# Linear attention and a routed feed-forward in one kernel: sixteen weight loads and three stores moved along one hand-written transfer queue, two tiles issued from a second one

## The chip, the cores and the metric

One Trainium2 chip, one of its cores. A time is the device time of one execution in microseconds (us), the median of the runs shown. TensorE is written PE, VectorE DVE, ScalarE ACT, GpSimd POOL; SP is the SyncE engine, which computes nothing here and only issues transfers.

## The reference, cut to what matters

q, k and v are (4, 8, 768, 64) in fp32: 4 batches, 8 heads, 768 positions, head size 64. Then a router takes the 128 best rows of each batch through a feed-forward with 1024 hidden units.

```python
for b in range(nb):                                   # blocks of 64 positions
    intra = einsum('bhic,bhjc->bhij', qb, kb) * Dmask # decayed causal scores
    intra = einsum('bhij,bhjd->bhid', intra, vb)
    inter = einsum('bhid,bhde->bhie', qb * lam_pow, kv_state)
    out[:, :, sl] = intra + inter
    kv_state = lam_block * kv_state + einsum('bhsd,bhse->bhde', kb * rev_pow, vb)
x = out.transpose(0, 2, 1, 3).reshape(B, S, 512)
scores = x @ w_gate
for b in range(B):
    top = argpartition(-scores[b], 128)[:128]
    ye = maximum(x[b, top] @ w1, 0) @ w2              # w1 512x1024, w2 1024x512
    out[b, top] = x[b, top] + sigmoid(scores[b, top])[:, None] * ye
```

## The kernel before, in words

**Groups.** The work is cut into 24 groups g of 128 positions, six for each batch. A group needs three tiles, kn, qn and vn (k, q and v of its positions, all heads), each 256 KB, read in pieces of 256 bytes. `load(g)` (L71) issues the three, in this order. The pool `ld` has six buffers of each, so `load(g)` has to wait until group g - 6 is done with its own.

**The main loop (L673).** Iteration g finishes group g and prepares group g + 1. Groups 0 to 8 run in a "wide" form (128 positions at a time), later ones in a narrow form (two halves of 64). On PE an iteration of the wide form goes: transposes of q and k of group g + 1 (L204); the state product of group g + 1 (L271, or L280 for the first narrow group; needs vn of g + 1, and k decayed by POOL, `kd`, L188); scores times v of group g (L335); scores of g + 1 (L231); the share of the state (L323); the row of gate scores (L405, once in each iteration).

**The feed-forward.** When a batch's six groups are done, its 128 rows are found, and POOL fetches them from the output in DRAM by an indirect transfer (`xs`, L480), so all six stores of that batch must have landed. `expert` then hands out pieces that stand between the narrow iterations: transposes of `xs` (L493), eight hidden chunks f = 0 to 7 (L530; chunks 0 to 3 need the first four weight transfers, chunks 4 to 7 the next four), eight output chunks (L542; each needs one of the last eight). The first batch's pieces begin in iteration 9.

**The transfers.** All loads, weights and stores of whole groups go through one queue, SP's, in the order in which the program issues them. The weights come as 16 transfers of 256 KB (rows of 2 KB), here called w0 to w15 (w1 in w0 to w7, w2 in w8 to w15). Where they stand is written out by hand: `WEIGHTS_WITH` (L50) names the groups behind whose kn or qn load the next weight is issued, and `STORES_WITH` (L51) the loads behind which the store of a finished group (L377, 256 KB) is issued. Stores not named there are issued when the group is finished. ACT's queue carries two small tensors at the start, `lam` and `w_gate` (L86, L88).

**The start.** Iteration -1 prepares group 0. PE transposes k, then q of group 0; ACT copies each out of PSUM (L208); DVE builds the decay masks; POOL makes an identity and a zero tile (L110 to L115), then decays k of groups 0 and 1.

Of the kernel before, what the change touches and what calls it, by code (L numbers as in the profile page):

```python
# [8 lines left out]
FP32 = mybir.dt.float32  # L9
# [8 lines left out]
def kernel(  # L18
# [12 lines left out]
    nc = tc.nc  # L31
# [5 lines left out]
    L = 128  # L37
# [8 lines left out]
    assert 0 <= CAP < S  # L46

    AHEAD = 6
    WIDE = 9
    WEIGHTS_WITH = {"kn": (12, 13, 14), "qn": range(4, 17), "vn": ()}  # L50
    STORES_WITH = {  # L51
        "kn": {5: (0,), 6: (1,), 7: (2,), 8: (3,), 9: (4, 5)}, "qn": {},
        "vn": {11: (6,), 12: (7,), 13: (8,), 14: (9, 10), 15: (11,), 20: (12, 13), 21: (14, 15)},
    }
    PIECES = {13: (1, 0, 1), 14: (1, 0, 1), 15: (1, 0, 2), 20: (1, 0, 1), 21: (1, 0, 1),
# [4 lines left out]
    const = ctx.enter_context(tc.tile_pool(name="const", bufs=1))  # L60
    ld = ctx.enter_context(tc.tile_pool(name="ld", bufs=AHEAD))
    att = ctx.enter_context(tc.tile_pool(name="att", bufs=3))
# [8 lines left out]
    def load(g):  # L71
        b, c = divmod(g, NT)
        rows = slice(c * L, (c + 1) * L)
        tiles = []
        for name, src in (("kn", k), ("qn", q), ("vn", v)):
            t = ld.tile([128, H, D], FP32, name=name)
            nc.sync.dma_start(out=t[:], in_=src[b, :, rows, :].rearrange("h p d -> p h d"))
            tiles.append(t)
            if g in WEIGHTS_WITH[name]:
                weights.pop(0)()  # L80
            for s in STORES_WITH[name].get(g, ()):
                store(s)
        loaded[g] = tiles
# [2 lines left out]
    nc.scalar.dma_start(out=lam_b[:], in_=lam.unsqueeze(0).broadcast_to([128, H]))  # L86
    wg_row = const.tile([1, HD], FP32, name="wg_row")
    nc.scalar.dma_start(out=wg_row[:], in_=moe_w_gate.unsqueeze(0))  # L88
    for g in range(3):
        load(g)  # L90
    wg_b = const.tile([128, HD], FP32, name="wg_b")
# [15 lines left out]
    weights = [w1_load(f0, n, c) for f0 in (0, n) for c in range(NDC)]  # L107
    weights += [w2_load(f) for f in range(NFC)]

    ident = const.tile([128, 128], FP32, name="ident")  # L110
    make_identity(nc, ident)
    zero = const.tile([128, L], FP32, name="zero")
    nc.gpsimd.memset(zero[:], 0.0)
    one_row = const.tile([1, 128], FP32, name="one_row")
    nc.gpsimd.memset(one_row[:], 1.0)  # L115

    su = psum.tile([128, 2, 512], FP32, name="su")
    o_ = psum.tile([128, 2, 512], FP32, name="o")
# [18 lines left out]
    for hp in range(NHP):  # L137
        for hh in range(2):
            h = 2 * hp + hh
            nc.vector.tensor_tensor_scan(  # L140
                out=mask_w[:, hh, hp, :], data0=lam_b[:, h : h + 1].broadcast_to([128, L]),
# [38 lines left out]
    def wide(g):  # L180
        return g < WIDE

# [192 lines left out]
    def store(g):  # L375
        b, t = divmod(g, NT)
        nc.sync.dma_start(  # L377
            out=out[b, t * L : (t + 1) * L, :],
            in_=x_bs[b][:, t].rearrange("p a b e -> p (a b e)"),
        )  # L380
# [261 lines left out]
    def products(n):  # L642
        for _ in range(min(n, len(pieces))):
            pieces.pop(0)()

    def ahead(g):
        return min(4 + max(0, (g - 12) // 2), AHEAD)

# [4 lines left out]
    def loads_to(n):  # L653
        while next_load[0] < min(n, NG):
            load(next_load[0])
            next_load[0] += 1
# [16 lines left out]
    for g in range(-1, NG):  # L673
        loads_to(g + ahead(g))
        if g < 0:
# [9 lines left out]
                out=decay_w[:], in_=qpow[:, :, L - 1 : L].broadcast_to([128, NHP, D])  # L685
# [57 lines left out]
        now = PIECES.get(g, (1, 1, 1))  # L743
        if g == WIDE:
            products(1)
# [101 lines left out]
```

## Time and profile before

| what | value |
|---|---|
| median of 3 runs | 176.89 us (176.65 to 179.35) |
| the profiled execution's own time | 177.37 us |
| its span, first to last instruction | 175.6 us |
| busy share of the span: PE, DVE, POOL, ACT | 91%, 56%, 52%, 41% |
| moved by transfers | 31.96 MB, 182 GB/s over the span |
| mean granted TensorE clock | 0.989 |

All rows come from one profiled execution. A time in a row is counted from the span's start. The profiled execution took 0.48 us more than the median; 1.8 us of its time lies outside the span. Busy shares are averages over stages that have different limits, so the stage of the change has to be looked at by itself.

### The profile page before, as it was taken

To read this page: it belongs to the slowest core of one execution; us is meant where nothing else is said; L and a number is where in the kernel's file an instruction comes from. 1 tells how busy PE (TensorE), PEld (TensorE's weight loads), DVE (VectorE), ACT (ScalarE), POOL (GpSimd) and SP (SyncE) were. 2 spreads that over 40 slices of the span, in tenths; PEclk is the share of its full clock that TensorE was granted. 3 is DMA by queue.
4 is the path that set the end of the run, shared out by engine and by line. 5 is a ranking of instruction groups with operands and counts; after the bars stand their busy time and mean duration, and the time that the engine had idled before them with its cause. 6 is when DMAs were issued, how large, how long until landed. Compare 5 with 4: busy or idle time off the path is not lost.

```text
span 175.6 us, 7861 instructions
## 1 busy us (share of the span) xinstructions
PE 160.3 (91%) x3440; PEld 132.5 (75%) x3440; DVE 98.4 (56%) x227; ACT 71.9 (41%) x192; POOL 91.4 (52%) x101
## 2 busy tenths in 40 slices
PE   6798999873998999999999899999999999989990
PEld 6568888763887899966667799966668888459970
DVE  2577866772595475458546754757567956340011
ACT  2244465541244465454444446544546445003100
POOL 2259974445287842654975953466776800220022
PEclk9999999997899999999999999999999999999999
DMA  4999999998999999999999979999503111021000
GB/s 93 217 219 181 238 228 248 260 231 211 267 234 256 214 295 283 270 276 260 239 240 218 244 168 260 289 241 229 171 14 113 66 63 60 0 60 63 0 30 30
DMA packets 81475, 31.96 MB, mean 182 GB/s; under 512 B 75809, under 2 KB 75809, under 8 KB 81442
## 3 DMA queue, kind: packets, MB, share of 16 engines
q1 hardware_dynamic: 80640, 29.37, 71.2%
q0 software_dynamic: 656, 2.10, 3.7%
q8 instruction: 27, 0.44, 1.1%
q14 instruction: 6, 0.05, 0.1%
q10 hardware_dynamic: 146, 0.01, 0.0%
HBM read 24.12 MB, written 7.34 MB: 179 GB/s over the span
## 4 chain that ended last, share of the span: by engine, by line
PE 75%; DMA 11%; DVE 4%; issue 3%; ACT 2%; SPq 2%; POOLq 1%
PE m L530 18%; PE m L542 13%; PE m L204 10%; PE o L323 6%; PE o L343 5%; PE su L238 4%; PE su L280 4%; PE o L335 4%; DMA vn<-in_v_dram 4%; DMA xs<-out_dram,tok 4%; DMA qn<-in_q_dram 3%; PE m L271 2%; PE m L567 2%; PE su L231 2%; DVE xg L385 2%
## 5 line engine op out<-in xcount | busy, mean ns | idle before, releaser
L530 PE MATMUL m<-xsT,w_sb 128*128 128x128 f32 x256 | 33.8, 281 | 0.5 <-ACT xsT L500 0.5
L415 DVE SCALAR_TENSOR_TENSOR table<-sc_row,sc,lead 128x128 bf16<-128x128 f32 (+5 forms) x24 | 24.8, 1033 | 15.4 <-ACT sc_row L408 14.8
L530 PEld LDWEIGHTS m<-xsT,w_sb 128*128 128x128 f32 x256 | 30.5, 192 | 1.2 <-ACT xsT L500 0.7
L218 POOL TENSOR_TENSOR qs<-qT,qpow 128x512 f32<-128x512 f32 x15 | 20.9, 1391 | 15.0 <-ACT qT L208 14.9
L385 DVE CUSTOM_DVE_ANT_0 xg<-x_b,wg_b 128x512 f32<-128x512 f32 x24 | 22.3, 930 | 9.1 <-ACT x_b L365 8.5
L542 PE MATMUL m<-w_sb,hs 128*128 128x512 f32 x48 | 25.0, 623 | 0.0
L293 POOL TENSOR_TENSOR decayed<-state,decay 128x256 f32<-128x256 f32 x25 | 18.9, 757 | 11.5 <-DVE state L312 10.6
L208 ACT COPY qT<-m 128x512 f32<-128x512 f32 x24 | 14.0, 585 | 11.4 <-PE m L204 9.1
L312 DVE TENSOR_TENSOR state<-su,decayed 128x256 f32<-128x256 f32 x25 | 10.6, 423 | 14.4 <-PE su L280 7.4
L534 ACT ACTIVATE hs<-m 128x128 f32<-128x128 f32 x32 | 8.9, 277 | 23.5 <-PE m L530 23.5
L188 POOL TENSOR_TENSOR kd<-kn,kpow 128x512 f32<-128x512 f32 x15 | 15.7, 1049 | 0.0
L188 POOL TENSOR_TENSOR kd<-kn,kpow_w 128x512 f32<-128x512 f32 x9 | 9.4, 1049 | 11.6 <-DMA kn<-in_k_dram 6.4
L323 PE MATMUL o<-state,qs 64*64 64x64 f32 x672 | 15.4, 224 | 0.0
L208 ACT COPY kT<-m 128x512 f32<-128x512 f32 x24 | 14.2, 592 | 2.6 <-PE m L204 2.6
L204 PE MATMUL m<-ident,qn 128*128 128x128 f32 x96 | 14.7, 275 | 0.6 <-DMA qn<-in_q_dram 0.5
L204 PE MATMUL m<-ident,kn 128*128 128x128 f32 x96 | 14.5, 273 | 0.0
L323 PEld LDWEIGHTS o<-state,qs 64*64 64x64 f32 x672 | 12.5, 134 | 2.5 <-issue 2.3
L408 ACT COPY sc_row<-m 128x128 f32<-128x128 f32 x24 | 6.3, 264 | 18.7 <-PE m L405 18.7
L216 POOL TENSOR_TENSOR qs<-qT,qpow 128x512 f32<-128x512 f32 x7 | 9.3, 1330 | 8.1 <-ACT qT L208 8.0
L204 PEld LDWEIGHTS m<-ident,qn 128*128 128x128 f32 x96 | 11.0, 141 | 2.6 <-issue 1.6
L343 PEld LDWEIGHTS o<-vn,p 64*64 64x64 f32 x480 | 8.5, 134 | 5.9 <-issue 3.0
L248 DVE TENSOR_TENSOR p<-su,mask_w 128x1024 f32<-128x1024 f32 x9 | 10.9, 1216 | 1.8 <-PE su L231 1.8
(85 smaller groups left out, 255.2 us busy)
## 6 DMA issues: line engine op xcount, KB each, us to landing
kn<-in_k_dram SPq DMA_DIRECT2D x24, 256.0 KB, 5.3
qn<-in_q_dram SPq DMA_DIRECT2D x24, 256.0 KB, 5.5
vn<-in_v_dram SPq DMA_DIRECT2D x24, 256.0 KB, 5.1
out_dram<-x_b SPq DMA_DIRECT2D x24, 256.0 KB, 4.2
w_sb<-in_moe_w_dram SPq DMA_DIRECT2D x16, 256.0 KB, 5.3
xs<-out_dram,tok POOLq DMA_INDIRECT x4, 4.0
out_dram<-y,tok POOLq DMA_INDIRECT x3, 4.1
out_dram<-y_half,half_at POOLq DMA_INDIRECT x2, 2.4
```

What stands on the lines that cost most here:

```text
L188: nc.gpsimd.tensor_tensor(out=kd[:], in0=loaded[g][0][:], in1=pw[:].rearrange("p a b -> p (a b)").unsqueeze(2).broadcast_to([128, H, D]), ...
L204: nc.tensor.transpose(tp[:, hp * L : (hp + 1) * L], in_=t[:, 2 * hp : 2 * hp + 2, :], identity=ident[:])
L208: nc.scalar.copy(out=dst[:].rearrange("p a i -> p (a i)"), in_=tp[:])
L218: nc.gpsimd.tensor_tensor(out=qs[:].rearrange("p a (c i) -> p a c i", c=2), in0=qTs[g].rearrange("p a (c i) -> p a c i", c=2), in1=qpow[:, ...
L248: nc.vector.tensor_tensor(out=p[:], in0=su[:], in1=mask_w[:].rearrange("p a b i -> p a (b i)"), op=ALU.mult,)
L293: nc.gpsimd.tensor_tensor(out=t[:], in0=states[n][:], in1=(decay_w if wide(g) else decay)[:], op=ALU.mult)
L323: nc.tensor.matmul(o_[half[c if wide(g) else hh ^ c], hh, hp * D : (hp + 1) * D], lhsT=qs[half[hh], hp, half[c]], rhs=states[n][half[hh], ...
L343: nc.tensor.matmul(o_[half[hh ^ c], hh, hp * D : (hp + 1) * D], lhsT=p[half[c], hh, hp * C : (hp + 1) * C], rhs=vn[half[c], 2 * hp + hh, : ...
L385: nc.vector.tensor_tensor_reduce(out=xg[:], in0=x_bs[b][:, t].rearrange("p a b e -> p (a b e)"), in1=wg_b[:], scale=1.0, scalar=0.0, op0=A ...
L415: nc.vector.scalar_tensor_tensor(out=table[:, : (t + 1) * L], in0=rows_[b][:, : (t + 1) * L], scalar=scs[b][:, t : t + 1], in1=lead[:, (NT ...
L530: nc.tensor.matmul(ph, lhsT=w1_sb[:, dc, f * 128 : (f + 1) * 128], rhs=keep["xsT"][:, dc, :], start=(dc == 0), stop=(dc == NDC - 1),)
L542: nc.tensor.matmul(py[:], lhsT=keep["hs"][:, f, :], rhs=w2_sb[:, f, :], start=(f == 0), stop=(f == NFC - 1),)
```

## The change

The order of SP's queue is rewritten, and two loads leave it.

- Weights: none with groups 4 to 6 any more. w0 to w3 go behind qn of groups 7 to 10 (before: 4 to 7), w4 and w5 behind kn and qn of group 11, w6 and w7 both behind kn of group 12, and so on; w15 goes behind kn of group 16 (before: behind its qn).
- Stores of groups 0, 1 and 2 go behind kn of groups 6, 7 and 8 (before: 5, 6 and 7). Stores 3, 4 and 5 keep their places (behind kn of 8, 9 and 9).
- vn of group 0 and kn of group 1 are issued from ACT's queue instead of SP's.
- ACT gets a copy of one column of the zero tile ahead of those two issues, so that its activation table is loaded by then. For that the POOL set-up moves ahead of the loads in the program's text.

```diff
+    FROM_ACT = (("vn", 0), ("kn", 1))
     WIDE = 9
-    WEIGHTS_WITH = {"kn": (12, 13, 14), "qn": range(4, 17), "vn": ()}
+    WEIGHTS_WITH = {
+        "kn": {11: 1, 12: 2, 13: 1, 14: 1, 15: 1, 16: 1},
+        "qn": {g: 1 for g in range(7, 16)}, "vn": {},
+    }
     STORES_WITH = {
-        "kn": {5: (0,), 6: (1,), 7: (2,), 8: (3,), 9: (4, 5)}, "qn": {},
+        "kn": {6: (0,), 7: (1,), 8: (2, 3), 9: (4, 5)}, "qn": {},
         "vn": {11: (6,), 12: (7,), 13: (8,), 14: (9, 10), 15: (11,), 20: (12, 13), 21: (14, 15)},
     }
...
-            nc.sync.dma_start(out=t[:], in_=src[b, :, rows, :].rearrange("h p d -> p h d"))
+            queue = nc.scalar if (name, g) in FROM_ACT else nc.sync
+            queue.dma_start(out=t[:], in_=src[b, :, rows, :].rearrange("h p d -> p h d"))
             tiles.append(t)
-            if g in WEIGHTS_WITH[name]:
+            for _ in range(WEIGHTS_WITH[name].get(g, 0)):
                 weights.pop(0)()
...
     nc.scalar.dma_start(out=wg_row[:], in_=moe_w_gate.unsqueeze(0))
-    for g in range(3):
-        load(g)
...
     ident = const.tile([128, 128], FP32, name="ident")
     make_identity(nc, ident)
     zero = const.tile([128, L], FP32, name="zero")
     nc.gpsimd.memset(zero[:], 0.0)
     one_row = const.tile([1, 128], FP32, name="one_row")
     nc.gpsimd.memset(one_row[:], 1.0)
+    warm = const.tile([128, 1], FP32, name="warm")
+    nc.scalar.copy(out=warm[:], in_=zero[:, :1])
+    for g in range(3):
+        load(g)
```

## Rows read from the trace of the kernel before

**Rows 1.** The profile's page: PE's busy share; then clock, transfers, rate in 40 slices.

```profile
PE 160.3 (91%) x3440; PEld 132.5 (75%) x3440; DVE 98.4 (56%) x227; ACT 71.9 (41%) x192; POOL 91.4 (52%) x101
...
PEclk9999999997899999999999999999999999999999
DMA  4999999998999999999999979999503111021000
GB/s 93 217 219 181 238 228 248 260 231 211 267 234 256 214 295 283 270 276 260 239 240 218 244 168 260 289 241 229 171 14 113 66 63 60 0 60 63 0 30 30
```

**Rows 2.** Waits of PE, longest first: total us, times, longest us.

```profile
PE m L271 <- DMA vn<-in_v_dram: 3.1, 2, 2.9
```

**Rows 3.** The chain that ended last: start us, length us, what.

```profile
1.24 4.91 DMA qn<-in_q_dram
...
35.56 6.57 DMA vn<-in_v_dram
```

**Rows 4.** Timeline of PE, 38 to 58 us: start, length, line, names, idle before.

```profile
38.21 0.32 PE L405 MATMUL m<-ident,sc 128*128 128x128 f32 x1 [0.78 <-DVE sc L385]
...
42.26 1.12 PE L271 MATMUL m<-vn,kd 128*64 128x64 f32 x16 [2.86 <-DMA vn<-in_v_dram]
43.14 1.95 PE L335 MATMUL o<-vn,p 128*64 128x64 f32 x32
...
47.01 0.32 PE L405 MATMUL m<-ident,sc 128*128 128x128 f32 x1
...
48.65 1.10 PE L335 MATMUL o<-vn,p 128*64 128x64 f32 x32
...
51.53 0.32 PE L405 MATMUL m<-ident,sc 128*128 128x128 f32 x1
...
52.72 0.69 PE L280 MATMUL su<-vn,kd 64*64 64x64 f32 x32
...
57.40 0.66 PE L493 MATMUL m<-ident,xs 128*128 128x128 f32 x4 [0.47 <-DMA xs<-out_dram,tok]
```

**Rows 5.** Busy time by engine in two stretches; then granted clock, transfer share, GB/s.

```profile
40.00:45.00 5.00, 2.74 (x48) 2.67 (x48) 0.72 (x3) 0.13 (x1) 3.12 (x3) 0.69 0.79 204
45.00:50.00 5.00, 5.00 (x138) 4.46 (x140) 4.22 (x8) 2.12 (x5) 1.48 (x2) 0.97 1.01 257
```

**Rows 6.** Tile vn of group 9: when issued, and how long to landing.

```profile
L77 SPq DMA_DIRECT2D vn<-in_v_dram x1: 382/382/382, 48.0 to 48.0; - x1
...
DMA to landing us min/median/max: 4.4/4.4/4.4
```

**Rows 7.** kn of group 12: its issue on SP's timeline, its time to landing.

```profile
59.80 0.38 SPq L77 DMA_DIRECT2D kn<-in_k_dram  x1
...
kn<-in_k_dram SPq DMA_DIRECT2D x1, 256.0 KB, 4.4
```

**Rows 8.** Timeline of PE: first batch's hidden chunk f = 4.

```profile
66.48 1.06 PE L530 MATMUL m<-xsT,w_sb 128*128 128x128 f32 x8
```

**Rows 9.** Tile vn of group 15: when issued, and how long to landing.

```profile
L77 SPq DMA_DIRECT2D vn<-in_v_dram x1: 382/382/382, 81.6 to 81.6; - x1
...
DMA to landing us min/median/max: 5.0/5.0/5.0
```

**Rows 10.** Timeline of PE: state product of group 15.

```profile
89.16 0.65 PE L280 MATMUL su<-vn,kd 64*64 64x64 f32 x32
```

**Rows 11.** Timeline of the start, all engines.

```profile
1.77 1.28 ACT L208 ACT_TABLE_LOAD   x1 [1.77 <-issue]
1.87 1.77 SPq L77 DMA_DIRECT2D vn<-in_v_dram  x1
...
5.68 0.59 ACT L208 COPY kT<-m 128x512 f32<-128x512 f32 x1 [2.63 <-PE m L204]
...
8.62 1.04 POOL L188 TENSOR_TENSOR kd<-kn,kpow_w 128x512 f32<-128x512 f32 x1 [0.78 <-DMA kn<-in_k_dram]
9.60 0.69 PE L271 MATMUL m<-vn,kd 128*64 128x64 f32 x16
...
11.61 0.69 PE L271 MATMUL m<-vn,kd 128*64 128x64 f32 x16 [0.31 <-issue]
```

More of the change, by code (lines that the diff above doesn't have):

```diff
@@ L88 @@
     nc.scalar.dma_start(out=wg_row[:], in_=moe_w_gate.unsqueeze(0))
+    ident = const.tile([128, 128], FP32, name="ident")
+    make_identity(nc, ident)
+    zero = const.tile([128, L], FP32, name="zero")
+    nc.gpsimd.memset(zero[:], 0.0)
+    one_row = const.tile([1, 128], FP32, name="one_row")
+    nc.gpsimd.memset(one_row[:], 1.0)
+    warm = const.tile([128, 1], FP32, name="warm")
+    nc.scalar.copy(out=warm[:], in_=zero[:, :1])
     for g in range(3):
@@ L108 @@
     weights += [w2_load(f) for f in range(NFC)]
[L110 to L115, printed above, removed]
     su = psum.tile([128, 2, 512], FP32, name="su")
```

## The prediction, made before the changed kernel ran

> **What bounds the kernel now.** I read the page first, then PE's waits, then the timeline around the largest one. PE is busy 91% of the span, and the transfers run at nine tenths or more from the second slice to about 120 us [rows 1]. Two resources are near their limits at once, so a stall removed on one may be given back on the other. PE's list of waits has one large entry: the state product L271 waits for vn, nearly all of it in one place [rows 2]. The chain of waits shows the same transfer, issued at 35.56, landing 6.57 us later at 42.1 [rows 3]. On the timeline it is vn of group 7, in iteration 6 [rows 4]: PE is ready at 42.26 - 2.86 = 39.40 and starts at 42.26. [...] Measured from L405 to L405, that iteration takes 47.01 - 38.21 = 8.80 us and the next 51.53 - 47.01 = 4.52 [rows 4]. **What the stall costs is 8.80 - 4.52 = 4.28 us**, the lower clock included.
>
> **The new order, and the stall itself.** I counted transfers in the order of the program, ACT's two included. A 256 KB transfer at the 228 to 295 GB/s of the slices from 18 to 70 us (leaving out the dips to 211 and 214) takes 0.89 to 1.15 us [rows 1]; weights, stores and loads are all 256 KB. vn of group 7 is transfer 31 before (24 loads, 4 weights, 3 stores) and 27 after (24, 1, 2). Four fewer take 3.6 to 4.6 us: it would land at 37.5 to 38.6, ahead of the 39.40 at which PE asks. So this wait goes, and the clock's part with it.
>
> **What is late next.** The weights and stores taken out have to be sent later. Three places, each with PE's time moved 4.28 us earlier as long as nothing else holds it:
>
> - vn of group 9 is transfer 42 before and 39 after, three weights fewer. It landed at 48.0 + 4.4 = 52.4 [rows 6]; less 2.7 to 3.5 us it lands at 48.9 to 49.7. PE asks at 52.72 - 4.28 = 48.4 [rows 4]. A new stall of 0.5 to 1.3 us.
> - w7, without which hidden chunk 4 can't start, becomes transfer 52: behind kn of group 12, with a second weight beside it. Before, transfer 52 was kn of group 12. Up to and with it both orders hold the same 37 loads, 8 weights and 7 stores, so w7 should land when that one did: 59.80 + 4.4 = 64.2 [rows 7]. Chunk 4 started at 66.48 [rows 8]. **PE can be at most 66.48 - 64.2 = 2.3 us earlier there**; at 4.28 us earlier it would wait 2.0.
> - vn of group 15 is transfer 74 in both orders, with the same 48 loads, 15 weights and 11 stores ahead of it or in it. It landed at 81.6 + 5.0 = 86.6 [rows 9] and was needed at 89.16 [rows 10]: at most 2.5 us.
>
> The second and third don't add to the first, since they are dates that PE meets later or not at all. The tightest is w7. After group 17 no weights are left in SP's queue, so the loads run ahead until the buffers stop them, and what is gained stays to the end. Of the 4.28 us some 2.0 is given back, in one or more waits between 48 and 66 us.
>
> **The stores.** Those of groups 4 and 5 become transfers 35 and 36, earlier than before (38 and 39), so the fetch of `xs`, which needs them, can move up with PE. It was only 0.47 us late before [rows 4] and is not the tighter bound. I cost this at nothing; if the fetch did not move at all, L493 would be held at 57.4 and the whole gain would be gone (in the third rival).
>
> **The two loads on ACT.** ACT loads its table at 1.77 to 3.05 already, waiting for nothing, and its first real work is the copy at 5.68 [rows 11]. So the extra copy only fills idle time; a first-column copy is at most the 0.59 us of that whole-tile copy. It ends by 3.6 us. SP's own issue of vn of group 0 took 1.77 us [rows 11]. Two issues at 0.4 to 1.8 each keep ACT until 4.1 to 7.2, so the copy at 5.68 is late by 0 to 1.5 us; I take 0, since ACT's queue holds nothing else then. The landing is bounded the same way. q of group 0 took 4.91 us from issue [rows 3]; of that 1.2 is its own 256 KB at the 217 GB/s of the second slice [rows 1], and 3.7 is everything else. At the full rate kn of group 1, second on ACT's queue and issued near 4, lands at 4 + 3.7 + 2.4 = 10.1; at half the rate, shared with SP, at 12.5. It is wanted at 11.61 - 1.04 = 10.6, for the POOL product ahead of L271 [rows 11]. (vn of group 0, first on that queue and issued near 3.6, lands at 8.5 to 9.7 and is wanted at 9.60 [rows 11], so kn decides.) PE is therefore 0 to 1.9 us late at the start, the upper end being nearer, as SP keeps sending. I take 1.0. That costs nothing in the end: PE has 2.0 us in hand until w7's date, so a late start only shortens the waits there. At the upper end it still does (1.9 against 2.0). Nor does an early start help: group 0's q is still SP's second transfer.
>
> [...] No row here shows two queues at work, and the second rival holds that case.
>
> **The sum.** 4.28 for the stall, less 2.0 that the fixed dates take back, is 2.3 us. The profiled execution would go from 177.37 to 175.1; it stands 0.48 above the median, so the median goes from 176.89 to 174.6.
>
> **Rivals.**
>
> 1. *Forecast, stream-bound: 174.6 us, 55%.* Its own range is a gain of 1.3 to 2.9 (a 256 KB transfer more or less ahead of w7 is about 1 us; the 0.6 upward also holds the 2.5 of group 15): 174.0 to 175.6.
> 2. *The transfers keep up: 173.0 us, 18%.* The stream is faster than before. For: in 40 to 45 us, while PE stood, it fell to 204 GB/s against 257 in the next stretch [rows 5], worth 5 x (1 - 204/257) = 1.0 us; and four early transfers at 295 instead of 217 GB/s, with two queues at work, would save 4 x (1.2 - 0.89) = 1.2. Together 2.2 would nearly cancel what is given back: gain 3.2 with one, 4.3 with both, 172.6 to 173.7. Against: the dips are spread over the whole run, not only where PE stood, and the table of slices shows others at 181 and 211 [rows 1].
> 3. *Bound elsewhere: 176.3 us, 19%.* One more dip of about 1 us falls ahead of w7, or the fetch of `xs`, which runs among the loads, takes longer, or the loads alone go at the 217 GB/s of the beginning (nine loads of groups 3 to 5 at 1.2 instead of the 1.07 of 245 GB/s: 1.2 us). Gain 0 to 1.2: 175.7 to 176.9.
> 4. *Slower: 179.3 us, 8%.* ACT's queue is starved while SP's stays full. At a quarter of the 217 GB/s each of its two loads takes 4.8 us instead of 1.2: kn of group 1 lands at 4 + 3.7 + 9.6 = 17.3, 6.7 us after it is wanted. It decides from the point at which this exceeds the 4.28 us of the removed stall, a landing after 14.9. At a quarter the end is 6.7 - 4.28 = 2.4 later: 179.3. For and against: no row shows two full queues side by side, and half the rate is the plainer guess.
>
> That the change doesn't do what it says has no room for the order, which the program text fixes; for the table it would change nothing, as it is loaded early already.
>
> **How the numbers follow.** The predicted time is the first case's, 174.6. The range is 172.8 to 176.6: it takes in the first case, most of the second and most of the third, and leaves out the fourth and the ends. A measurement of this kernel can tell about 2% from no change, that is 3.5 us. Only the upper part of the second case gains that much (under 173.4): 14%. Slower by over 2% (180.4) is the tail of the fourth: 2%. The rest, 84%, lies within 2%.
>
> **What the changed profile would show.** Right: no wait of L271 for vn in iteration 6, the clock at nine tenths throughout 40 to 45 us; iterations 4.4 to 4.6 us long up to iteration 7; then shorter waits, for vn of group 9 near 48 to 50 us and for a weight before hidden chunk 4 near 64; w7 landing at 64.2 and vn of group 15 at 86.6, as their equal places before. Wrong: these two land more than 1 us earlier (second case), or the stall at 40 is split over vn of groups 7 to 10 with the same sum (third), or PE waits more than 4 us before 20 us (fourth). My forecast hangs most on the claim that equal composition means equal landing.

## The result, and the profile after

| | before | after |
|---|---|---|
| median (lowest to highest), 12 runs each | 176.92 us (175.37 to 179.35) | 174.97 us (172.99 to 177.33) |
| ratio after to before, 95% interval | | 0.9882 [0.9844, 0.9920] |
| profiled execution, its span | 177.37 us, 175.6 us | 177.33 us, 175.5 us |

The kernel is 1.2% faster: 1.95 us by the medians, where 2.3 were forecast. All ratios here compare undisturbed runs alone, so they can differ from the quotient of two medians. The profiled execution of the changed kernel took the longest of its twelve, 2.4 us above the median; its rows show where time goes, not how much of it in the end.

The page after, the same lines as [rows 1]:

```profile
PE 161.3 (92%) x3440; PEld 133.1 (76%) x3440; DVE 100.8 (57%) x227; ACT 72.1 (41%) x193; POOL 92.6 (53%) x101
...
PEclk9999999999999999999999999999999999999998
DMA  3999899999899998999999998984302111021000
GB/s 68 281 247 231 193 235 230 260 264 263 196 268 291 291 292 222 255 305 270 242 214 225 262 271 244 223 200 120 120 31 100 63 63 60 0 60 63 0 30 30
```

The dip of the clock in the tenth and eleventh slice is gone, and in the second and third slice the stream moves 281 and 247 GB/s, where [rows 1] have 217 and 219. The forecast has no such thing; the second rival has.

Waits of PE after, those of which the text speaks (against [rows 2]):

```profile
PE su L287 <- issue: 1.5, 2, 1.3
...
PE m L500 <- DMA xs<-out_dram,tok: 0.7, 1, 0.7
...
PE o L350 <- issue: 0.6, 1, 0.6
```

No wait for vn, none for a weight. What stands high in the list instead is "issue": PE stood inside a run of one line's instructions, and no semaphore ended it. The timeline of PE after, against [rows 4] and [rows 8] (lines have moved by 7: L405 is L412, L271 is L278, L280 is L287, L493 is L500, L530 is L537):

```profile
37.81 0.32 PE L412 MATMUL m<-ident,sc 128*128 128x128 f32 x1 [0.20 <-DVE sc L392]
...
39.05 0.69 PE L278 MATMUL m<-vn,kd 128*64 128x64 f32 x16
...
42.63 0.32 PE L412 MATMUL m<-ident,sc 128*128 128x128 f32 x1
...
47.63 0.32 PE L412 MATMUL m<-ident,sc 128*128 128x128 f32 x1 [0.41 <-issue]
...
48.81 0.69 PE L287 MATMUL su<-vn,kd 64*64 64x64 f32 x32
...
53.44 0.66 PE L500 MATMUL m<-ident,xs 128*128 128x128 f32 x4 [0.72 <-DMA xs<-out_dram,tok]
...
58.44 0.38 PE L350 MATMUL o<-vn,p 64*64 64x64 f32 x9 [0.64 <-issue]
...
63.48 1.06 PE L537 MATMUL m<-xsT,w_sb 128*128 128x128 f32 x8
...
69.78 0.50 PE L287 MATMUL su<-vn,kd 64*64 64x64 f32 x18 [1.33 <-issue]
```

Iteration 6 takes 42.63 - 37.81 = 4.82 us instead of 8.80: the stall is gone, and 3.96 us of it are still there when `xs` is transposed (57.40 before, 53.44 now) and 3.00 at chunk 4 (66.48, 63.48). The clock agrees; granted clock is the third number from the end, against [rows 5]:

```profile
40.00:45.00 5.00, 4.85 (x139) 4.25 (x137) 3.91 (x7) 1.92 (x4) 4.01 (x4) 1.00 0.91 251
```

But w7 landed far from its date of 64.2. Its issue after, and its time to landing: 56.27 + 4.57 = 60.84.

```profile
L111 SPq DMA_DIRECT2D w_sb<-in_moe_w_dram x1: 1246/1246/1246, 56.3 to 56.3; - x1
...
DMA to landing us min/median/max: 4.6/4.6/4.6
```

vn of group 9 landed at 47.35 (forecast 48.9 to 49.7), vn of group 7 at 34.35 (37.5 to 38.6). So the stream runs 1.6 to 4.3 us ahead of its forecast from early on, and what is kept is still no more than forecast. By the prediction's own signs this is its second case (w7 more than 1 us early) without that case's gain. Both had to be explained.

### The profile page after: what moved, and what is told of

It is laid out like the page before. It is cut to its first block, busy times and chain, and to the rows that moved or that the text cites. A ratio compares the mean times of both kernels' runs of the same rounds, so it can differ in the third digit from the quotient of the medians.

```text
span 175.5 us, 7863 instructions
## 1 busy us (share of the span) xinstructions
PE 161.3 (92%) x3440; PEld 133.1 (76%) x3440; DVE 100.8 (57%) x227; ACT 72.1 (41%) x193; POOL 92.6 (53%) x101
## 4 chain that ended last, share of the span: by engine, by line
PE 80%; DVE 5%; DMA 5%; issue 5%; ACT 3%; POOLq 1%; POOL 0%
PE m L537 18%; PE m L549 13%; PE m L211 11%; PE o L330 6%; PE o L350 5%; PE su L245 4%; PE su L287 4%; PE o L342 4%; DMA xs<-out_dram,tok 4%; PE m L278 3%; PE m L141 2%; DVE xg L392 2%; PE m L412 2%; PE m L574 2%; PE su L238 2%
## 5 line engine op out<-in xcount | busy, mean ns | idle before, releaser
L422 DVE SCALAR_TENSOR_TENSOR table<-sc_row,sc,lead 128x128 bf16<-128x128 f32 (+5 forms) x24 | 26.5, 1103 | 14.8 <-ACT sc_row L415 14.2
L537 PE MATMUL m<-xsT,w_sb 128*128 128x128 f32 x256 | 34.0, 281 | 0.7 <-ACT xsT L507 0.5
L537 PEld LDWEIGHTS m<-xsT,w_sb 128*128 128x128 f32 x256 | 30.5, 192 | 1.5 <-ACT xsT L507 0.7
L225 POOL TENSOR_TENSOR qs<-qT,qpow 128x512 f32<-128x512 f32 x15 | 21.0, 1400 | 13.8 <-ACT qT L215 13.8
L195 POOL TENSOR_TENSOR kd<-kn,kpow 128x512 f32<-128x512 f32 x15 | 16.2, 1080 | 0.0
L223 POOL TENSOR_TENSOR qs<-qT,qpow 128x512 f32<-128x512 f32 x7 | 9.8, 1405 | 6.9 <-ACT qT L215 6.9
L287 PE MATMUL su<-vn,kd 64*64 64x64 f32 x432 | 10.7, 219 | 1.6 <-issue 1.5
```

Of the source, the lines that this page charges most:

```text
L195: nc.gpsimd.tensor_tensor(out=kd[:], in0=loaded[g][0][:], in1=pw[:].rearrange("p a b -> p (a b)").unsqueeze(2).broadcast_to([128, H, D]), ...
L225: nc.gpsimd.tensor_tensor(out=qs[:].rearrange("p a (c i) -> p a c i", c=2), in0=qTs[g].rearrange("p a (c i) -> p a c i", c=2), in1=qpow[:, ...
L287: nc.tensor.matmul(su[half[hh], c, NHP * C + hp * D : NHP * C + (hp + 1) * D], lhsT=kd[half[c], h, :], rhs=vn[half[c], h, :], start=True, ...
L422: nc.vector.scalar_tensor_tensor(out=table[:, : (t + 1) * L], in0=rows_[b][:, : (t + 1) * L], scalar=scs[b][:, t : t + 1], in1=lead[:, (NT ...
L537: nc.tensor.matmul(ph, lhsT=w1_sb[:, dc, f * 128 : (f + 1) * 128], rhs=keep["xsT"][:, dc, :], start=(dc == 0), stop=(dc == NDC - 1),)
```

## The experiments

The loads are rows of 256 bytes, the weights rows of 2 KB. In 5 to 13 us only loads run, so there the time of one 256-byte packet can be read: a queue's share of the 16 engines' time, times 16 x 8 us, by its packets. Transfers in 5 to 13 us, before and then after; q1 is SP's queue, q10 ACT's:

```profile
DMA packets 6929, 1.75 MB, mean 218 GB/s; under 512 B 6929, under 2 KB 6929, under 8 KB 6929
...
q1 hardware_dynamic: 6929, 1.75, 130.4%
```

```profile
DMA packets 8360, 2.11 MB, mean 264 GB/s; under 512 B 8360, under 2 KB 8360, under 8 KB 8360
...
q1 hardware_dynamic: 6371, 1.61, 88.7%
q10 hardware_dynamic: 1989, 0.50, 27.7%
```

Before, a packet took 1.304 x 128 / 6929 = 24.1 ns; after, 0.887 x 128 / 6371 = 17.8 ns, on ACT's queue 0.277 x 128 / 1989 = 17.8 too. The same packets became shorter. But only those of the start: in the kernel before, too, a packet takes 0.892 x 24 / 1182 = 18.1 ns in 18 to 19.5 us, where again only loads run:

```profile
DMA packets 1183, 0.32 MB, mean 210 GB/s; under 512 B 1182, under 2 KB 1182, under 8 KB 1182
...
q1 hardware_dynamic: 1182, 0.30, 89.2%
```

Counted by the single packets of 256 bytes, before has 18.0 ns in 2 to 4 us, 22 to 25 ns in each 2 us from 4 to 16, and a mean of 19.0 from 20 to 130 us, where after has 18.1. Twelve microseconds at 24 instead of 18 ns are, by estimate, 3 us of the stream: about the lead that had to be explained. Why the long packets end near 16 us isn't shown.

Three parts of the change could shorten these packets: the order, the second queue, the extra copy. Four kernels, run on one chip, take the change apart.

**order_only**, the new order and the copy, nothing on ACT's queue (of the sixteen weights fifteen change places; w14 stays behind qn of group 15):

```diff
-    FROM_ACT = (("vn", 0), ("kn", 1))
+    FROM_ACT = ()
```

> The new order of weights and stores alone; v of group 0 and k of group 1 stay on SP's queue. First theory (transfers on ACT's queue add no bandwidth, the date of a transfer follows from its place and what is ahead of it): same time as the changed kernel, about 175.0 us, v of group 7 landing at 34 to 35 us as there. Second theory (two queues at work in the first 10 us carry more, and the whole stream is 3 us ahead from then on): v of group 7 lands near 37.5 to 38.5, still before PE asks, but later weights and v of group 9 are late; 175.5 to 176.3 us.

Measured: 0.9858 [0.9765, 0.9950], median 175.98 (before, on that chip: 177.68). Packets of 17.8 ns, 239 GB/s in 5 to 13 us, vn of group 7 at 34.93. The second queue is not needed for the faster stream.

**act_only**, the old order, the two loads on ACT, no copy (against before):

```diff
+    FROM_ACT = (("vn", 0), ("kn", 1))
...
-            nc.sync.dma_start(out=t[:], in_=src[b, :, rows, :].rearrange("h p d -> p h d"))
+            queue = nc.scalar if (name, g) in FROM_ACT else nc.sync
+            queue.dma_start(out=t[:], in_=src[b, :, rows, :].rearrange("h p d -> p h d"))
```

> The old order; only v of group 0 and k of group 1 go to ACT's queue, without the extra copy. First theory: 176.9 us, v of group 7 lands at 42 as before. Second theory: v of group 7 lands about 3 us earlier, near 39, so that the stall of iteration 6 (2.9 us and the lower clock behind it) is mostly gone; 173.5 to 175.5 us.

Measured: 0.9952 [0.9897, 1.0007], median 178.24. Packets of 23.3 ns, 220 GB/s, vn of group 7 at 42.52, and the stall stays, in three pieces:

```profile
PE m L273 <- DMA vn<-in_v_dram: 2.6, 3, 1.7
```

**no_warm**, the whole change but for the one-column copy (against after):

```diff
-    warm = const.tile([128, 1], FP32, name="warm")
-    nc.scalar.copy(out=warm[:], in_=zero[:, :1])
```

> The changed kernel without the one-column copy ahead of ACT's two issues. If the copy is worth nothing: 175.0 us, the table load still over before the first copy of k at 5 to 7 us. Rival: the table load falls behind the issues and makes the first copy late, 175.3 to 176 us.

Measured: 1.0026 [0.9965, 1.0087], median 177.84. The whole gain hangs on the copy, and the packets are long again; transfers in 5 to 13 us:

```profile
DMA packets 6947, 1.75 MB, mean 219 GB/s; under 512 B 6947, under 2 KB 6947, under 8 KB 6947
...
q1 hardware_dynamic: 4947, 1.25, 89.6%
q10 hardware_dynamic: 2000, 0.50, 37.7%
```

That is 23.2 and 24.1 ns. The copy itself is over at 3.24 us, before these packets begin. What it leaves behind is its tile: it takes 32 bytes of each partition of SBUF, and all tiles allocated later begin 32 bytes further on. In the built programs the q, k and v tiles begin 224 bytes past a multiple of 256 in before, act_only and no_warm, and at a multiple of 256 in after, order_only and half_weights. At the old place the dates of the forecast come true to about 1 us. Waits of PE in no_warm:

```profile
PE su L285 <- DMA vn<-in_v_dram: 0.8, 1, 0.8
...
PE m L535 <- DMA w_sb<-in_moe_w_dram: 0.3, 1, 0.3
```

vn of group 7 landed at 37.92, vn of group 9 at 50.11 with a stall of 0.8, w7 at 65.16 with one of 0.3.

**half_weights**, the whole change with 8 of the 16 weight transfers left out:

```diff
-        "kn": {11: 1, 12: 2, 13: 1, 14: 1, 15: 1, 16: 1},
-        "qn": {g: 1 for g in range(7, 16)}, "vn": {},
+        "kn": {11: 1, 12: 2}, "qn": {g: 1 for g in range(7, 12)}, "vn": {},
...
-    weights = [w1_load(f0, n, c) for f0 in (0, n) for c in range(NDC)]
-    weights += [w2_load(f) for f in range(NFC)]
+    weights = [w1_load(f0, n, c) for f0 in (0,) for c in range(NDC)]
+    weights += [w2_load(f) for f in range(n)]
...
```

(Not shown: in three products of the feed-forward `f` becomes `f % n`.)

> The changed kernel with 8 of the 16 weight transfers left out; hidden chunks 4 to 7 and output chunks 4 to 7 use the weights of chunks 0 to 3, so the feed-forward's values differ, PE's instructions don't. If the gain of 4.3 us at iteration 6 is given back because the transfers are too dense afterwards (a late weight, or gaps of PE for which no semaphore is responsible): about 172.5 us, and those gaps between 50 and 95 us shrink. If PE itself gives it back whatever the transfers do: 175.0 us and the same gaps.

Measured: 0.9846 [0.9773, 0.9919], median 174.80. Its interval holds that of the change almost whole: 2 MB fewer to move bring nothing that can be told. That is near the 175.0 us of the second case in its expectation. What remains in its waits of PE is "issue":

```profile
PE su L244 <- issue: 1.3, 1, 1.3
PE o L349 <- issue: 1.2, 1, 1.2
```

**pad32, pad64, pad96, after_pad32.** Now the address by itself: an unused tile of 32, 64 or 96 bytes, behind `wg_row` in the kernel before and in the changed one. POOL fills it once.

```diff
+    pad = const.tile([128, 8], FP32, name="pad")
+    nc.gpsimd.memset(pad[:], 0.0)
```

(16 and 24 columns in pad64 and pad96; 8 in after_pad32.)

> The kernel before plus one unused tile of 32 bytes per partition behind w_gate's row (zeroed by POOL); nothing else changed. It moves every later tile in SBUF up by 32 bytes, as the one-column tile of the change does, so that q, k and v tiles start at a multiple of 64 (and 256) instead of 32 past one. Third theory (the place of the tiles decides how fast a 256 KB load lands): loads of the start land every 1.03 to 1.06 us instead of 1.20, v of group 7 lands near 38, the stall of iteration 6 is gone; 173.5 to 175.5 us. Second theory (two queues): nothing moves, 177 us and 42.

> The control: the same unused tile with 64 bytes, so that the tiles stay 32 past a multiple of 64. Third theory: loads of the start every 1.20 us, v of group 7 near 42, 177 us, as before. If any shift of the addresses helps, or the extra POOL instruction does: like the 32-byte tile.

> The same unused tile with 96 bytes: q, k and v tiles start at a multiple of 64 that isn't one of 128 or 256 (64 past a multiple of 256), weights at a multiple of 256. If 64 is what counts: as with 32 bytes, loads every 1.03 to 1.06 us. If a row of 256 bytes must start at a multiple of 256: loads every 1.2 us, 177 us.

> The whole change plus an unused tile of 32 bytes, which puts the tiles back to 32 past a multiple of 64; the copy ahead of ACT's issues stays. Third theory: loads of the start every 1.2 us, and the time of the change without its one-column tile: 176.5 to 177.5 us, ratio to before about 1.00; the new order has to pay its dates (w7 landing at 64 to 65). If the copy itself mattered: 175.0 us, ratio 0.988.

Measured on one chip (before: 178.74), with the place of the q, k and v tiles past a multiple of 256 bytes:

| kernel | place | packet in 5 to 13 us, both queues | ratio to before | median |
|---|---|---|---|---|
| pad32 | 0 | 17.8 ns | 0.9777 [0.9713, 0.9840] | 174.61 |
| pad64 | 32 | 23.9 ns | 0.9999 [0.9938, 1.0061] | 178.41 |
| pad96 | 64 | 23.6 ns | 0.9918 [0.9847, 0.9988] | 177.83 |
| after_pad32 | 32 | 24.4 ns | 1.0052 [0.9993, 1.0111] | 178.63 |

Transfers in 5 to 13 us, pad32 and then pad64:

```profile
q1 hardware_dynamic: 7902, 1.99, 110.0%
```

```profile
q1 hardware_dynamic: 6917, 1.74, 129.1%
```

An unused tile makes the kernel before 2.2% faster (1.5% in the repeat below), and the same tile takes from the change all that it had. pad64 has the same POOL instruction as pad32, on twice the columns, and nothing changes: not the fill but the address counts. vn of group 7 landed at 37.44 in pad32; the waits of its profiled execution (177.03 us, well above its median) still name later loads of vn, 2.3 us in L282. In after_pad32 vn of group 7 landed at 39.11 and w7 at 66.63, later than the 64 to 65 expected, and the waits of PE have the late transfers back:

```profile
PE m L213 <- DMA qn<-in_q_dram: 1.8, 3, 1.1
...
PE su L289 <- DMA vn<-in_v_dram: 1.3, 3, 0.8
PE m L280 <- DMA vn<-in_v_dram: 1.0, 1, 1.0
```

**after_again, pad32_again, align_all, pad160.** Two are repeats, for the comparison of the change with the bare address. align_all has 96 bytes behind `wg_row` and 192 more behind the tile `place_i` in the kernel before, so that the weights begin at a multiple of 256 too. pad160 has 40 columns: loads at 128, weights at 64.

```diff
+    pad = const.tile([128, 24], FP32, name="pad")
+    nc.gpsimd.memset(pad[:], 0.0)
...
+    pad2 = const.tile([128, 48], FP32, name="pad2")
+    nc.gpsimd.memset(pad2[:], 0.0)
```

> The changed kernel once more, beside the three others on one chip. Its ratio to the kernel before should again be 0.985 to 0.992.

> The kernel before with the unused 32-byte tile, once more, beside the changed kernel. If the change's whole gain is the place of its tiles and its new order and second queue are worth nothing: the same ratio as the changed kernel or lower, 0.978 to 0.990. If the new order gives something of its own: 0.5% to 1% above the changed kernel.

> The kernel before with two unused tiles, 96 bytes behind w_gate's row and 192 bytes behind the last constant, so that the weights too start at a multiple of 256 (with the 32-byte tile they are 192 past one). If a 2 KB row that starts off a multiple of 256 costs time as a 256-byte row does: weights land every 0.6 to 0.7 us instead of 0.76 and the time is 0.5 to 1 us under the 32-byte tile's. If only the short rows of q, k and v matter: the same as the 32-byte tile.

> The kernel before with one unused tile of 160 bytes: q, k and v tiles 128 past a multiple of 256. If 128 is enough: loads of the start every 1.03 to 1.06 us, about 250 GB/s from 3 to 13 us, ratio 0.975 to 0.990. If a row of 256 bytes has to start at a multiple of 256: every 1.2 us, 224 GB/s, ratio 0.99 to 1.00 as with 96 bytes.

Measured on one chip (before: 177.89):

| kernel | loads, weights begin at | packet in 5 to 13 us, both queues | ratio to before | median |
|---|---|---|---|---|
| after_again | 0, 192 | 17.8 ns | 0.9915 [0.9862, 0.9967] | 176.39 |
| pad32_again | 0, 192 | 17.8 ns | 0.9848 [0.9773, 0.9923] | 174.15 |
| align_all | 0, 0 | 17.8 ns | 0.9895 [0.9808, 0.9981] | 175.56 |
| pad160 | 128, 64 | 24.0 ns | 0.9944 [0.9898, 0.9991] | 176.29 |

Aligned weights add nothing that can be told. The bare address is as good as the whole change, by both medians better (174.61 and 174.15, against 174.97 and 176.39). The two that ran on one chip have overlapping ratios, but these share the runs of before; set directly against each other, after_again is 1.4 us above pad32_again (an estimate from the 9 and 6 runs that the ratios use, 95% interval 0.3 to 2.4). That is one chip, and against align_all, which has the same place for its loads, the difference is 0.6 us and not clear of zero. So the new order isn't shown to add anything at the aligned place, and may cost. The bare address beats the kernel before in both, and is the version to keep. pad32_again by its page and its timeline of PE, against [rows 1] and [rows 4]:

```profile
PE 161.2 (94%) x3440; PEld 133.1 (77%) x3440; DVE 98.3 (57%) x227; ACT 72.0 (42%) x192; POOL 92.5 (54%) x102
```

```profile
38.02 0.32 PE L407 MATMUL m<-ident,sc 128*128 128x128 f32 x1 [0.20 <-DVE sc L387]
...
39.26 0.69 PE L273 MATMUL m<-vn,kd 128*64 128x64 f32 x16
...
42.84 0.32 PE L407 MATMUL m<-ident,sc 128*128 128x128 f32 x1
```

vn of group 7 in pad32_again, its issue and its time to landing:

```profile
L77 SPq DMA_DIRECT2D vn<-in_v_dram x1: 385/385/385, 32.7 to 32.7; - x1
...
DMA to landing us min/median/max: 5.2/5.2/5.2
```

With the old order, and not one weight moved, vn of group 7 lands at 37.89 instead of 42.1 and the stall is gone; its list of PE's waits names no transfer. The busy times of PE, DVE, ACT and POOL are within 1.2% of those before: it isn't the engines that became faster. The tiles from which the stores read move by the same 32 bytes; their part, if any, was not separated from that of the loads. **Where the gain goes** is seen in the row of gate scores (L405 before), once in each iteration, in us against the profiled execution of before; negative is earlier:

| iteration | 4 | 6 | 8 | 10 | 13 | 15 | 20 | 23 |
|---|---|---|---|---|---|---|---|---|
| after | 0.33 | -4.38 | -3.96 | -1.41 | -1.15 | -0.68 | 0.54 | -0.05 |
| order_only | 0.39 | -4.33 | -4.14 | -2.36 | -2.10 | -1.08 | -1.07 | -1.07 |
| no_warm | 0.57 | -4.14 | -2.57 | -1.85 | -1.85 | -0.78 | -0.21 | -0.44 |
| half_weights | 0.06 | -4.65 | -3.51 | -3.10 | -3.10 | -2.83 | -2.83 | -2.84 |
| pad32_again | 0.54 | -4.17 | -4.37 | -4.36 | -3.88 | -4.85 | -2.90 | -3.50 |

Each is one execution, and those of one kernel differ by some 3 us in the end (pad32 ended at -0.36, pad32_again at -3.50). What repeats is iteration 6, after which every kernel here stands 4.1 to 4.7 us ahead. What follows doesn't.

## Why the prediction was right in size and wrong in cause

**The stall, 4.28 us: right.** Iteration 6 became 3.98 us shorter, and [rows 4] against the timeline after give 4.38 from the row at 47.01 to the one at 42.63. The granted clock of 40 to 45 us, 0.69 in [rows 5], was 1.00 after, and the product of 1.95 us behind the stall (L335 in [rows 4], L342 after) took 1.13: the lower clock that the 4.28 includes was gone with the wait. Iterations 6 and 7 took 4.82 and 5.00 us, a little over the 4.4 to 4.6 forecast. At the old address the landing came at 37.92 in no_warm, inside the forecast 37.5 to 38.6, and at 39.11 in after_pad32, 0.5 past it: counting transfers works about as well as their speed stays.

**"Equal composition means equal landing": wrong for this kernel, nearly right for its order at the old address.** In no_warm vn of group 9, w7 and vn of group 15 landed at 50.11, 65.16 and 85.90 (forecast to 49.7, 64.2, 86.6), with waits of 0.8 and 0.3 us where they were foreseen; in after_pad32 the first two came at 51.69 and 66.63, 2 us late and more. In the changed kernel w7 landed at 60.84 and PE waited for no weight. The premise that broke is the next point's.

**The extra copy "only fills idle time": the step that failed.** It was costed by its time on ACT, which is right: 0.19 us, ended at 3.24.

```profile
1.76 1.28 ACT L101 ACT_TABLE_LOAD   x1 [1.76 <-issue]
1.82 0.47 ACTq L82 DMA_DIRECT2D vn<-in_v_dram  x1
2.31 0.60 ACTq L82 DMA_DIRECT2D kn<-in_k_dram  x1
3.05 0.19 ACT L101 COPY warm<-zero 128x1 f32<-128x1 f32 x1
```

(Timeline of ACT after.) What wasn't looked at is that the copy needs a tile, and that this tile moved all later ones by 32 bytes. With the change's order and queues held, its 32 bytes decide between 0.9882 and 1.0026; alone they give 0.9777 and 0.9848. That it is the address is shown by pad32 (0.9777) against pad64 (0.9999) and by after_pad32 (1.0052). Why loads to the places off a multiple of 256 are slower isn't shown. In 5 to 13 us their packets took 23.3 to 24.4 ns, against 17.8 at a multiple of 256, and the distance past it made no difference that shows: 32, 64, 128 and 224 cost the same to about 1 ns. From 20 to 130 us the means are 19.1, 18.4, 18.3 and 19.0 ns for 32, 64, 128 and 224 (pad64, pad96, pad160, before), against 18.1 aligned.

**The two loads on ACT.** Forecast 1.0 us late at the start, hidden later; it was 0.31 (iteration 0 against before; pad32_again, with no load moved, stood 0.52 late there), and the two issues did not even wait for the table load beside which they stand. kn of group 1 landed at 9.11 in no_warm, ahead of the forecast 10.1 to 12.5. That a second queue brings no bandwidth, which the forecast's dates assume, no row of before shows; at the old address two brought none (219 to 221 GB/s in no_warm, act_only and after_pad32, 218 or 219 with one). At the aligned one they carried 264 and 256 in the two runs of the change, against 239 to 249 with one; in the time no difference can be told (order_only 0.9858, after 0.9882).

**`xs` costed at nothing: right.** It moved up with PE, by 3.96 us, and the wait grew from 0.47 to 0.72.

**"What is gained stays to the end": wrong.** With no load and no weight late, 3.9 us (after) and 3.1 us (order_only) are given back behind iteration 8 all the same; in half_weights and pad32_again it is 0.7 and 0.9. At the old address no_warm stands 2.57 ahead at iteration 8, as the dates allow, and 0.44 at the end. In the changed kernel the largest steps are at the "issue" entries: 0.64 at 58.44 and 1.33 at 69.78, about half of what it gives back; the rest is in smaller steps. order_only has two larger ones (its waits, then its timeline):

```profile
PE o L350 <- issue: 3.5, 2, 2.0
```

```profile
96.64 0.28 PE L350 MATMUL o<-vn,p 64*64 64x64 f32 x3 [2.00 <-issue]
```

These entries have a pattern. The fourteen traces have fourteen such pauses over 0.6 us, eight of them in after, order_only, no_warm and half_weights. Count from 0 all that the profile lists of PE: multiplications, weight loads and its 79 to 81 semaphore instructions and drains, 6961 in all in the changed kernel. All eight then stand at place 193 or 194 of a block of 256 (2498, 3009, 2498, 4289, 4289, 1985, 2242, 4289), and so do four of the other six (the two that don't are 0.85 us at 142.40 in act_only and 0.65 at 50.31 in pad96). The profile also lists 27 transfers of 16 KB each on a queue that it calls instruction. To 27 transfers there are 6961 / 27 = 258 of PE's instructions for each, and in blocks of 256 the 6961 make 27.2:

```profile
q8 instruction: 27, 0.44, 1.1%
```

Each of the twelve pauses ends 1.3 to 1.5 us after one of these transfers does; the one that ends at 69.78 follows the longest of its run, 65.83 to 68.37. And in every trace, for every n from 1 to 25 (the first block is block 0), PE reaches place 193 of block n at least 1.19 us after the nth of these transfers has ended, while it reaches place 192, one instruction before, up to 0.87 us ahead of that end. From this the author infers that PE waited for its own program there, up to 2.00 us in one pause. It rests on the pattern alone: no run moved the blocks or took these transfers away. That half_weights, with 2 MB less, still has three such pauses speaks against the mere volume of transfers as what makes such a transfer late.

**The rivals.** The second case named the effect, a faster stream, with the wrong cause (it had two queues at work in mind) and with a gain of 3.2 to 4.3 that didn't come (its own terms give 3.3 with one of them). That the forecast gain and the measured one lie 0.35 us apart is luck, a meeting of two errors: an effect of the tile's 32 bytes that was costed at nothing, and a loss later on that was costed at nothing too. Without the 32 bytes the change as it was understood gained nothing that can be told (1.0026 in no_warm, 1.0052 in after_pad32).

**Open:** what makes a transfer of instructions late in one execution and not in the next, if that is what PE waits for; why the long packets of unaligned tiles end after some 16 us; whether pad96 and pad160, whose loads are as slow as before in 5 to 13 us, get their 0.6 to 0.8% from the shorter packets that they have after 20 us (18.4 and 18.3 ns against 19.0); whether the new order costs time at aligned addresses, as after_again against pad32_again suggests.

## What to carry to other kernels

A new tile, however small, can move every tile behind it; here one column moved them by 32 bytes. Before costing a reordering of loads, compare the start addresses of their tiles and the time of one packet in both kernels, and try the bare shift as a control. If rows of 256 bytes are loaded, as here, try their tiles at multiples of 256 bytes first: that made a packet of 5 to 13 us 17.8 ns long instead of 23.3 to 24.4, and did at least as much as the whole change (0.9777 and 0.9848, against 0.9882 and 0.9915). When a stall on a tuned engine is removed, follow one row per iteration to the end, for the gain can be lost again: here 3.9 us (after) and 3.1 us (order_only), with no load and no weight late.

## What the runs showed of the hardware

- In 5 to 13 us, with loads of 256-byte rows alone, a packet took 17.8 ns and one queue carried 239 to 249 GB/s where the tiles begin at a multiple of 256 bytes of a partition; at 32, 64, 128 and 224 past it 23.3 to 24.4 ns and 218 to 221 GB/s, on one queue or two. Later the difference was small: from 20 to 130 us 18.1 against means of 18.3 to 19.1 ns.
- A one-column tile takes 32 bytes of a partition; these 32 bytes, unused, made the whole kernel 2.2 and 1.5% faster (pad32, pad32_again).
- PE stood for up to 2.00 us (order_only) without a wait that the profile shows. Of fourteen such pauses over 0.6 us twelve stand 193 or 194 instructions into a block of 256 and end 1.3 to 1.5 us behind the end of a 16 KB transfer on the queue called instruction.
- ACT's transfers were issued at 1.82 and 2.31 us while its table load ran from 1.76 to 3.04 (after).
